# Weight difference in quarters, shared evacuations and a new order of all queues in a fused recurrence and maxout kernel

## The chip, the cores and the metric

The kernel runs on one core of a Trainium2 chip. The metric is device time in microseconds (us) of one execution; lower is better. A profiled execution also has a span (first to last instruction), some 1.7 us shorter than its time. A run more than 1.5% above the fastest of its kernel is called slow and is left out of all ratios; the medians quoted are of all runs, slow ones included.

## The reference

A gated recurrence over 768 time steps, for 4 batches and 8 heads of width 48, feeds a feed-forward layer with a maximum of two products:

```python
for t in range(S):                      # S = 768, per batch and head
    state = f[t][:, None] * state + outer(k[t], v[t])      # f = sigmoid(f_logit)
    y[t] = q[t] @ state
x = y as (3072, 384)
g = maximum(x @ w1, x @ w2)             # w1, w2: 384 x 1024
out = g @ w_out                         # 1024 x 384
```

The kernel uses max(a, b) = b + relu(a - b): out = relu(x @ (w1 - w2)) @ w_out + x @ (w2 @ w_out). So it needs the **difference** wd = w1 - w2 and the **product of the weights** m2 = w2 @ w_out, both computed on the chip.

## The kernel before

The time axis is cut into three windows for each of four batches: twelve "steps". All work is a list of words, issued to the five engines, each of which gets its own words in that order. The order is therefore in essence the schedule.

```python
# Lf, Lk, Lq, Lv: loads (SyncE queue)   W1, W2: row gathers of w1, w2 (GpSimd queue)   Wo: load of w_out
# E: two exponential passes (ScalarE)   e/g: pair sums es (GpSimd/VectorE)   C: cumulative sums (TensorE)
# X: five exponentials (ScalarE)        K/k, Q/q: kp, qp products (GpSimd/VectorE)   V/U: vb cast
# T: transposes (TensorE) + trs copies  A: at products (TensorE) + masking at_m (VectorE)
# S, Y: y products, xT copies           D, N: sadd products and new state
# wc, wT, wo, wm: cast w2, transpose it, cast w_out, product m2   ws: difference wd
# d g.fp: layer piece (h, relu into gT) o g.par: output piece   (a letter v, a, p after w.. names the engine)
ORDER = """
... V1 D0 S0 K1 W1:1 W2:1 W2:2 E2 Lf:3 N0 g2 W1:2 Lk:2 Lq:2 q1 D1 Z0 Y0 T1 N1 E3 e3 A1 wTa0 C2 S1 Lv:2
wcp1 C3 Wo:0 Z1 wcv2 Wo:1 Lf:4 X2 wsv0 wsv1 Y1 q2 X3 k2 Lk:3 wTa1 Lv:3 Lq:3 V2 wTv2 d0.0 d0.1 d0.2
d0.3 Lf:5 T2 wov0 d1.0 d1.1 wov2 Lk:4 d1.2 woa3 A2 Lv:4 D2 d1.3 Lq:4 Lf:6 wop1 E4 wma2 Lk:5 wma0 N2
g4 Q3 k3 wmv1 ...                                                               # (cut)
"""
def stage_T(s):                                   # (cut: 32 transposes into two PSUM banks)
    for h in range(2):
        nc.vector.tensor_copy(t[:, h], ps[h])
def stage_Y_act(s):                               # (cut)
    for h, ps in enumerate(ys.pop(s)):
        nc.scalar.copy(x[:, :, :, h, :], ps.rearrange("p j (a t) -> p j a t", a=2))
    for r in range(2):                            # fill the free rows of xT with the fourth head pair
        nc.scalar.dma_start(out=x[r * DP + D:(r + 1) * DP, 0:KT, :], in_=x[r * DP:r * DP + D, KT, :])
def piece_d(g, fp):                               # uses columns 256 fp .. 256 fp + 255 of wd
    for f in range(2):
        ff = 2 * fp + f
        for kt in range(KT):
            nc.tensor.matmul(out=ps[:, f, :], lhsT=wd[:, kt, ff * C:(ff + 1) * C], rhs=xT[g][:, kt, :], ...)
    nc.scalar.activation(gT[g][:, 2 * fp:2 * fp + 2, :], ps, AF.Relu)
def make_m2(kt, copy):
    for ff in range(FG):
        nc.tensor.matmul(out=ps, lhsT=w2T[:, ff, kt * C:(kt + 1) * C], rhs=wo[:, ff, :], ...)
    copy(m2[:, kt, :], ps)
def subtract(h, engine):
    cols = slice(h * d_ff // 2, (h + 1) * d_ff // 2)
    engine.tensor_sub(wd[:, :, cols], w1_f[:, :, cols], w2_f[:, :, cols])
```

## Time and profile before

| | before |
|---|---|
| time, median of 3 | 147.72 us (147.45 to 148.41) |
| span of the profiled run | 146.0 us |
| first layer piece (first h matmul) | 32.16 us |
| from there to the last matmul | 109.94 us, 0.56 us of it idle on TensorE |
| last eviction and store | 3.90 us |

The last three rows add up to the span. The views that give them are shown in the prediction. In a list of instructions, a line reads: start, length, engine, source line, operation, output<-inputs, shapes, count, and in brackets the idle time before it and what ended it.

### The profile page before, as it was taken

Reading aid. Unit: us, or ns where it says so; the run is one execution under the profiler, and the core shown is the slowest. Engines: PE = TensorE matmul, PEld = TensorE weight load, DVE = VectorE, ACT = ScalarE, POOL = GpSimd, SP = SyncE. Lnnn points to the kernel's source line nnn. Section 1 sums busy time; section 2 is a strip of 40 time slices with the busy share of each in tenths; the row PEclk is TensorE's granted clock in tenths of the full one; section 3 lists DMA queues with packets and bytes.
Section 4 is the critical chain, followed back from the end, with each engine's and each line's share of the span. In section 5 each row is a group of like instructions: output and inputs, shape, how many; then the busy total and the mean of one; then the engine's idle time right before and its main releaser. Section 6 shows DMA issues by size and latency. Waiting matters only on the chain.

```text
span 146.0 us, 5288 instructions
## 1 busy us (share of the span) xinstructions
PE 123.3 (84%) x2292; PEld 90.6 (62%) x2292; DVE 95.4 (65%) x179; ACT 89.9 (62%) x179; POOL 57.9 (40%) x68
## 2 busy tenths in 40 slices
PE   0017379649999999999999999999999999999990
PEld 0005267437866767876867676786857877866750
DVE  5157988479797697867893868957588751613030
ACT  3462947774797786969967886586526634650500
POOL 7376777220019475544206748286305610000000
PEclk9999999999999999999999999999999999999998
DMA  3999999999999004999999994993002301102022
GB/s 103 325 326 354 355 357 408 399 316 264 299 259 268 7 14 136 315 318 292 264 292 274 278 245 150 277 277 111 27 8 104 121 6 47 77 14 108 4 108 108
DMA packets 55128, 29.25 MB, mean 200 GB/s; under 512 B 50624, under 2 KB 52800, under 8 KB 55104
## 3 DMA queue, kind: packets, MB, share of 16 engines
q1 hardware_dynamic: 52704, 25.17, 59.7%
q0 software_dynamic: 864, 3.15, 5.3%
q10 hardware_dynamic: 1536, 0.59, 1.5%
q8 instruction: 18, 0.29, 0.8%
q14 instruction: 6, 0.05, 0.1%
HBM read 23.59 MB, written 4.72 MB: 194 GB/s over the span
## 4 chain that ended last, share of the span: by engine, by line
PE 63%; DMA 11%; POOL 7%; ACT 6%; DVE 6%; issue 4%; DVEq 0%
PE h L360 22%; PE o L373 18%; PE o L370 7%; DMA w_f<-in_moe_w_dram,row_of 6%; PE trp L236 4%; PE y L306 3%; DMA qt<-in_q_dram 3%; PE at L252 3%; PE y L286 3%; POOL kp L219 2%; DMA ft<-in_f_logit_dram 2%; POOL w_f L102 2%; ACT both L180 2%; PE sadd L320 1%; DVE wd L405 1%
## 5 line engine op out<-in xcount | busy, mean ns | idle before, releaser
L362 ACT ACTIVATE gT<-h 128x512 bf16<-128x512 f32 x48 | 28.0, 598 | 22.1 <-PE h L360 19.9
L360 PE MATMUL h<-xT,wd 128*128 128x256 bf16 x288 | 36.9, 281 | 2.3 <-DVE wd L405 1.9
L373 PE MATMUL o<-wo,gT 128*128 128x384 bf16 x192 | 35.1, 326 | 0.0
L264 DVE TENSOR_TENSOR at_m<-at,mask 128x512 bf16<-128x512 f32 x48 | 29.8, 683 | 5.3 <-PE at L252 5.3
L360 PEld LDWEIGHTS <-wd 128*128 128x128 bf16 x288 | 28.0, 101 | 8.4 <-DVE wd L405 2.2
L375 DVE COPY ob<-o 128x384 f32<-128x384 f32 x24 | 13.3, 556 | 21.8 <-PE o L373 21.8
L373 PEld LDWEIGHTS <-gT 128*128 128x128 bf16 x192 | 18.8, 98 | 12.4
L337 POOL TENSOR_TENSOR state<-tmp_s,f_last 128x256 bf16<-128x256 f32 x16 | 10.5, 657 | 37.2 <-DVE tmp_s L336 24.6
L219 POOL TENSOR_TENSOR kp<-kt,f_inv 128x768 bf16<-128x768 f32 x9 | 16.3, 1815 | 10.3 <-DMA kt<-in_k_dram 5.9
L239 DVE COPY trs<-trp 128x1024 bf16<-128x1024 bf16 x24 | 15.4, 685 | 3.4 <-PE trp L236 3.4
L370 PE MATMUL o<-m,xT 128*128 128x384 bf16 x72 | 15.7, 328 | 0.0
L344 ACT CAST xT<-y 128x512 bf16<-128x512 f32 x24 | 12.9, 591 | 3.9 <-PE y L306 3.9
L210 ACT ACTIVATE f_inv<-cum 128x384 f32<-128x384 f32 x12 | 5.9, 493 | 13.9 <-DVE even L201 9.8
L187 POOL TENSOR_TENSOR es<-both 128x384 bf16<-128x384 f32 x9 | 9.0, 999 | 8.7 <-issue 4.4
L180 ACT ACTIVATE both<-ft 128x768 f32<-128x768 f32 x12 | 10.2, 846 | 3.6 <-DMA ft<-in_f_logit_dram 2.2
L219 POOL TENSOR_TENSOR qp<-qt,f_dec 128x768 bf16<-128x768 f32 x6 | 11.6, 1939 | 0.0
L195 PE MATMUL cum<-es,u_inc 128*128 128x384 bf16 x12 | 4.6, 380 | 7.4 <-POOL es L187 7.4
L181 ACT ACTIVATE both<-both 128x768 f32<-128x768 f32 x12 | 10.1, 844 | 0.4
L201 DVE TENSOR_TENSOR even<-cum,both 128x384 f32<-128x384 f32 x12 | 6.6, 552 | 5.7 <-PE cum L197 5.1
L252 PE MATMUL at<-trs 48*64 48x128 bf16 x384 | 9.2, 234 | 1.3 <-DVE trs L239 1.3
L336 DVE TENSOR_TENSOR tmp_s<-sadd,state 128x256 f32<-128x256 f32 x16 | 6.8, 422 | 4.8 <-POOL state L337 3.0
L286 PE MATMUL y<-trs,state 48*64 48x128 bf16 x160 | 7.0, 226 | 2.6 <-DVE state L333 2.6
(64 smaller groups left out, 154.5 us busy)
## 6 DMA issues: line engine op xcount, KB each, us to landing
ft<-in_f_logit_dram SPq DMA_DIRECT2D x12, 384.0 KB, 5.6
vt<-in_v_dram SPq DMA_DIRECT2D x12, 384.0 KB, 5.6
kt<-in_k_dram SPq DMA_DIRECT2D x12, 384.0 KB, 5.5
qt<-in_q_dram SPq DMA_DIRECT2D x12, 384.0 KB, 5.1
out_dram<-ob SPq DMA_DIRECT2D x12, 384.0 KB, 2.5
wo_f<-in_moe_w_out_dram SPq DMA_DIRECT2D x2, 768.0 KB, 12.6
xT<-xT ACTq DMA_DIRECT2D x24, 24.0 KB, 3.2
w_f<-in_moe_w_dram,row_of POOLq DMA_INDIRECT x6, 6.4
```

Of the source, the lines that this page charges most:

```text
L180: nc.scalar.activation(flat(both), flat(loaded[s]["f"]), AF.Exp, bias=0.0, scale=-1.0)
L219: engine.tensor_mul(pad(nm + "p", s)[:, :, :, 0:D], by_parity(loaded[s][nm]), t.rearrange("p two (h d) -> p two h d", h=H))
L239: nc.vector.tensor_copy(t[:, h], ps[h])
L252: nc.tensor.matmul(out=ps[r][h * HC:(h + 1) * HC, j % 2, par, :], lhsT=t[rows, h, 0, j, par, :], rhs=t[rows, h, 1, j].rearrange("p a t -> ...
L264: nc.vector.tensor_mul(m[:, r, 2 * jj:2 * jj + 2], ps[r], mask.rearrange("p j a b t -> p j a (b t)"))
L286: nc.tensor.matmul(out=ys[s][h][r * DP:(r + 1) * DP, j, :], lhsT=st[rows, j, :], rhs=t[rows, h, 1, j].rearrange("p a t -> p (a t)"), start ...
L344: nc.scalar.copy(x[:, :, :, h, :], ps.rearrange("p j (a t) -> p j a t", a=2))
L360: nc.tensor.matmul(out=ps[:, f, :], lhsT=wd[:, kt, ff * C:(ff + 1) * C], rhs=xT[g][:, kt, :], start=(kt == 0), stop=(kt == KT - 1))
L362: nc.scalar.activation(gT[g][:, 2 * fp:2 * fp + 2, :], ps, AF.Relu)
L370: nc.tensor.matmul(out=ps, lhsT=xT[g][:, kt, cols], rhs=m2[:, kt, :], start=(kt == 0), stop=False)
L373: nc.tensor.matmul(out=ps, lhsT=gT[g][:, ff, cols], rhs=wo[:, ff, :], start=False, stop=(ff == FG - 1))
L375: nc.vector.tensor_copy(obs[g][:, par, :], ps)
```

## The change

The stated intent: cut the difference into quarters, so that a piece waits only for the 256 columns it uses; let ScalarE and VectorE share some evacuations; compute m2 before the first piece; and reorder every queue.

```diff
 ORDER = """
-Lf:0 E0 Lv:0 e0 C0 X0 Lk:0 V0 W2:0 Lf:1 K0 Lq:0 Lv:1 E1 q0 e1 T0 Lk:1 C1 Lf:2 W1:0 Lq:1 A0 X1 wca0
-V1 D0 S0 K1 W1:1 W2:1 W2:2 E2 Lf:3 N0 g2 W1:2 Lk:2 Lq:2 q1 D1 Z0 Y0 T1 N1 E3 e3 A1 wTa0 C2 S1 Lv:2
-wcp1 C3 Wo:0 Z1 wcv2 Wo:1 Lf:4 X2 wsv0 wsv1 Y1 q2 X3 k2 Lk:3 wTa1 Lv:3 Lq:3 V2 wTv2 d0.0 d0.1 d0.2
+Lf:0 E0 Lv:0 g0 Lk:0 Lf:1 W2:0 W2:1 E1 Lq:0 C0 X0 wca0 k0 U0 Lf:2 Lk:1 Lq:1 q0 Lv:1 e1 C1 X1 W2:2 K1
+Q1 W1:0 T0 Lf:3 D0 A0 Wo:1 Wo:0 N0 Lk:2 Lq:2 Lv:2 V1 E2 Lf:4 g2 W1:1 wca1 t1 Lk:3 E3 e3 D1 C2 N1 A1
+X2 Lf:5 wTv1 wTv0 wov3 wov0 S0 wov1 wca2 W1:2 C3 Z0 Lq:3 S1 Lv:3 Lk:4 woa2 Z1 Y0 Lq:4 K2 y1 wTv2 X3
+wmv0 wsv0 wma1 q2 wma2 wsp2 wsv1 T2 U2 d0.0 d0.1 Lv:4 Lk:5 E4 D2 Lq:5 N2 wsv3 A2 S2 Lv:5 d0.2 d0.3
+e4 K3 d1.0 Z2 o0.0 V3 E5 Y2 C4 Lf:6 Q3 e5 o0.1 X4 T3 D3 d1.1 K4 N3 d1.2 C5 V4 X5 d1.3 Q4 A3 d2.0 Q5
   (the rest of the list is reordered in the same way: cut)
-    def stage_T(s):
+    def stage_T(s, copy=nc.vector.tensor_copy):
-        for h in range(2):
-            nc.vector.tensor_copy(t[:, h], ps[h])
+        nc.vector.tensor_copy(t[:, 0], ps[0])
+        copy(t[:, 1], ps[1])
-    def stage_Y_act(s):
+    def stage_Y_act(s, copy=nc.scalar.copy):
-        for h, ps in enumerate(ys.pop(s)):
-            nc.scalar.copy(x[:, :, :, h, :], ps.rearrange("p j (a t) -> p j a t", a=2))
+        for h, (ps, fn) in enumerate(zip(ys.pop(s), (nc.scalar.copy, copy))):
+            fn(x[:, :, :, h, :], ps.rearrange("p j (a t) -> p j a t", a=2))
-    def subtract(h, engine):
-        cols = slice(h * d_ff // 2, (h + 1) * d_ff // 2)
+    def subtract(part, engine):
+        cols = slice(part * d_ff // 4, (part + 1) * d_ff // 4)
+        "t": lambda a: stage_T(int(a), nc.scalar.copy),                  # trs shared, 4 steps
+        "y": lambda a: (stage_Yv(int(a)), stage_Y_act(int(a), nc.vector.tensor_copy)),   # xT shared, 7 steps
```

More of the change, by code (lines that the diff above doesn't have):

```diff
@@ L17 @@
 ORDER = """
-Lf:0 E0 Lv:0 e0 C0 X0 Lk:0 V0 W2:0 Lf:1 K0 Lq:0 Lv:1 E1 q0 e1 T0 Lk:1 C1 Lf:2 W1:0 Lq:1 A0 X1 wca0
-V1 D0 S0 K1 W1:1 W2:1 W2:2 E2 Lf:3 N0 g2 W1:2 Lk:2 Lq:2 q1 D1 Z0 Y0 T1 N1 E3 e3 A1 wTa0 C2 S1 Lv:2
-wcp1 C3 Wo:0 Z1 wcv2 Wo:1 Lf:4 X2 wsv0 wsv1 Y1 q2 X3 k2 Lk:3 wTa1 Lv:3 Lq:3 V2 wTv2 d0.0 d0.1 d0.2
-d0.3 Lf:5 T2 wov0 d1.0 d1.1 wov2 Lk:4 d1.2 woa3 A2 Lv:4 D2 d1.3 Lq:4 Lf:6 wop1 E4 wma2 Lk:5 wma0 N2
-g4 Q3 k3 wmv1 C4 U3 S2 D3 Z2 N3 Lq:5 X4 o1.0 T3 E5 Y2 e5 o0.0 K4 C5 X5 A3 Lf:7 V4 S3 Q4 o0.1 T4 Z3
@@ L23 @@
-Lv:5 E6 Y3 Lf:8 D4 Lq:6 e6 Lk:6 N4 Lv:6 d2.0 o1.1 A4 K5 E7 S4 Z4 d2.1 Lq:7 d2.2 d2.3 Lf:9 Y4 V5 D5
-Lv:7 N5 d3.0 d3.1 g7 d3.2 C6 q5 Lf:10 o2.0 X6 K6 Lv:8 C7 X7 T5 o2.1 A5 S5 Lk:7 E8 Z5 e8 d3.3 U6 d4.0
-d4.1 C8 Y5 q6 q7 X8 Lk:8 K7 V7 o3.0 Lq:8 T6 d4.2 o3.1 d4.3 E9 E10 D6 e9 N6 A6 d5.0 o4.0 Lv:9 d5.1
-d5.2 d5.3 C9 e10 D7 N7 S6 Z6 Lf:11 X9 Lq:9 Lk:9 Lq:10 T7 Y6 Q8 o4.1 U9 Lk:10 A7 K8 V8 S7 o5.0 C10 Z7
-k9 E11 Lv:10 Y7 Lv:11 Lq:11 X10 D8 Q9 Lk:11 T8 o5.1 d6.0 d6.1 d6.2 A8 S8 Q10 D9 Z8 d6.3 d7.0 T9 Y8
@@ L28 @@
-o6.0 d7.1 K10 d7.2 A9 e11 T10 U10 d7.3 o6.1 C11 o7.0 X11 S9 Z9 D10 K11 A10 Y9 o7.1 d8.0 d8.1 d8.2
-V11 Q11 d8.3 S10 T11 Z10 D11 Y10 o8.0 d9.0 o8.1 d9.1 d9.2 d9.3 A11 S11 d10.0 Z11 d10.1 d10.2 Y11
-o9.0 d10.3 o9.1 o10.0 d11.0 d11.1 d11.2 d11.3 o10.1 o11.0 o11.1
+Lf:0 E0 Lv:0 g0 Lk:0 Lf:1 W2:0 W2:1 E1 Lq:0 C0 X0 wca0 k0 U0 Lf:2 Lk:1 Lq:1 q0 Lv:1 e1 C1 X1 W2:2 K1
+Q1 W1:0 T0 Lf:3 D0 A0 Wo:1 Wo:0 N0 Lk:2 Lq:2 Lv:2 V1 E2 Lf:4 g2 W1:1 wca1 t1 Lk:3 E3 e3 D1 C2 N1 A1
+X2 Lf:5 wTv1 wTv0 wov3 wov0 S0 wov1 wca2 W1:2 C3 Z0 Lq:3 S1 Lv:3 Lk:4 woa2 Z1 Y0 Lq:4 K2 y1 wTv2 X3
@@ new lines @@
+wmv0 wsv0 wma1 q2 wma2 wsp2 wsv1 T2 U2 d0.0 d0.1 Lv:4 Lk:5 E4 D2 Lq:5 N2 wsv3 A2 S2 Lv:5 d0.2 d0.3
+e4 K3 d1.0 Z2 o0.0 V3 E5 Y2 C4 Lf:6 Q3 e5 o0.1 X4 T3 D3 d1.1 K4 N3 d1.2 C5 V4 X5 d1.3 Q4 A3 d2.0 Q5
+Lf:7 d2.1 d2.2 D4 Lq:6 Lv:6 S3 Z3 V5 T4 Lq:7 N4 Lk:6 Lv:7 E6 d2.3 y3 o1.0 Lq:8 Lq:9 A4 K5 Lf:8 S4 Z4
+E7 e6 o1.1 C6 Y4 g7 D5 X6 T5 o2.0 Q6 Lk:7 C7 V6 N5 X7 o2.1 d3.0 Lf:9 d3.1 k6 d3.2 Lv:8 A5 D6 t6 d3.3
+N6 d4.0 d4.1 Q7 Lv:9 d4.2 d4.3 A6 S5 S6 Z5 E8 K7 Z6 y5 e8 V7 o3.0 o3.1 E9 Lf:10 D7 Lk:8 y6 Lk:9 C8
@@ L31 @@
+Lf:11 g9 o4.0 d5.0 N7 V9 Lv:10 X8 d5.1 C9 X9 V8 Lk:10 T7 o4.1 d5.2 Q8 d5.3 Lq:10 k8 K9 d6.0 t8 A7 D8
+o5.0 E10 Lv:11 S7 Z7 E11 A8 e10 q9 D9 Y7 o5.1 d6.1 d6.2 C10 d6.3 S8 e11 T9 Z8 X10 Lk:11 y8 o6.0 K10
+d7.0 d7.1 d7.2 Lq:11 q10 t10 A9 S9 U11 C11 d7.3 Z9 o6.1 o7.0 X11 y9 o7.1 Q11 U10 d8.0 K11 d8.1 d8.2
+d8.3 T11 D10 D11 A10 d9.0 d9.1 d9.2 o8.0 d9.3 A11 S10 Z10 S11 Z11 Y10 o8.1 y11 o9.0 o9.1 d10.0 d10.1
+d10.2 d10.3 d11.0 d11.1 d11.2 o10.0 d11.3 o10.1 o11.0 o11.1
 """
@@ L427 @@
         "V": lambda a: stage_V(int(a), nc.vector.tensor_copy), "U": lambda a: stage_V(int(a), nc.scalar.copy),
-        "T": attention(stage_T), "S": attention(stage_S), "Z": attention(stage_Z),
+        "T": attention(stage_T), "t": lambda a: stage_T(int(a), nc.scalar.copy),
+        "S": attention(stage_S), "Z": attention(stage_Z),
         "A": lambda a: (stage_A(int(a)), stage_A_dve(int(a))),
         "Y": lambda a: (stage_Yv(int(a)), stage_Y_act(int(a))),
+        "y": lambda a: (stage_Yv(int(a)), stage_Y_act(int(a), nc.vector.tensor_copy)),
         "D": lambda a: (stage_D(int(a)), stage_D_dve(int(a), 0)),
```

## The prediction

> **What bounds the kernel now.** I began with the page's busy row and its 40 slices, went on to the stretches (busy time by engine in chosen windows), then to the chain that ended last, and only then to the engines' timelines of the first 45 us.
>
> ```profile
> PE 123.3 (84%) x2292; PEld 90.6 (62%) x2292; DVE 95.4 (65%) x179; ACT 89.9 (62%) x179; POOL 57.9 (40%) x68
> ...
> PE   0017379649999999999999999999999999999990
> ...
> DMA  3999999999999004999999994993002301102022
> ```
>
> Busy shares are averages over two regimes. TensorE is filled in every slice from the tenth on and mostly empty before; the DMA is full from the second slice to the thirteenth. The cut by stretches, made at the start of the first layer piece (32.16 us) and at the end of the last matmul (142.10 us), says it exactly:
>
> ```profile
> 0.00:32.16 32.16, 13.93 (x316) 11.12 (x317) 20.60 (x52) 19.38 (x38) 18.95 (x35) 1.00 1.03 330
> 32.16:142.10 109.94, 109.38 (x1976) 79.51 (x1976) 74.29 (x127) 70.53 (x142) 38.92 (x33) 1.00 0.58 166
> 142.10:146.00 3.90, 0.00 (x0) 0.00 (x0) 0.56 (x1) 0.00 (x0) 0.00 (x0) 0.83 0.25 101
> ```
>
> The columns are the length, then busy us and count of PE, PEld, DVE, ACT and POOL, then clock, DMA share and GB/s. After 32.16 us TensorE idles 0.56 us in 110 us, so no engine there can be sped up to any effect. Before it TensorE has 18 us of idle time; after it stands a fixed end of 3.9 us (last eviction, last store). The chain shows what ends the empty stretch:
>
> ```profile
> 20.09 1.04 POOL w_f L102
> 21.14 0.63 POOL state L337
> 21.77 0.16 issue
> 21.93 8.14 DMA w_f<-in_moe_w_dram,row_of
> 30.07 0.03 issue
> 30.10 0.05 DVEq L405
> 30.15 0.04 issue
> 30.20 1.92 DVE wd L405
> 32.11 0.05 issue
> 32.16 4.37 PE h L360 x24
> ```
>
> The last gather of w1 is issued at 21.93 us, lands 8.14 us later, half of the weight difference is then subtracted in 1.92 us, and only then can the first piece (h) run. Everything TensorE does after that point, divided by its rate, is the rest of the kernel. One thing matters among it:
>
> ```profile
> 40.62 4.06 PE L399 MATMUL m2p<-wo,w2T 128*128 128x384 bf16 x24
> ```
>
> The product of the weights (w2 times w_out) is computed at 40.6 us, in the full stretch, although both its inputs were loaded by about 30 us.
>
> **What the skill says.** The Trainium skill, "TensorE: Matmul & The Clock Gate", Part 1, says that the array runs at half rate until it has been busy for some 3.4 us. The trace agrees: the first 24 h matmuls took 4.37 us, 182 ns each, while 18 later ones took 2.07 us in the chain, 115 ns each, and the page's clock row, which is the throttle's grant, shows nothing of it. "SBUF — State Buffer", Who interferes with whom, says VectorE with two SBUF inputs and GpSimd lock each other out for a whole instruction. The trace agrees: the qp product on VectorE takes 0.95 us as a rule, but 1.88 us at 10.10 us, where a kp product was running on GpSimd. "DMA: Bandwidth & Descriptors", Queues, rings and completion order, says engines take packets from the queues in turn, so a gather doesn't simply wait behind all queued loads. Here gathers landed in 5.3 to 8.4 us, the slow ones being those issued close together with the w_out load.
>
> **The change, part by part.** Nothing of the mathematics goes: 144 pairs of h matmuls, 24 o groups and all attention products stay.
>
> (1) **Product of the weights ahead of the pieces.** In the old order TensorE did, before the first piece, four cum products, two rounds each of transposes, at, sadd and both y products, and three w2 transposes. The new order has all of these too, and adds the three m2 products and the transposes of step 2. At the full rate these are 3 x 8 x 163 ns = 3.9 us (163 from 1.30 us per eight o matmuls in the chain; the trace shows about 4.06 us) and 0.57 us (the chain's transposes of one step). So at the first piece about 4.5 us less work remains.
>
> (2) **A warmer array.** The cold part of the first pieces costs 4.37 - 24 x 0.109 = 1.75 us (0.109 from 2.62 us per 24 late in the chain). In the new order the 24 products of 384 columns stand just before; they absorb the cold part, in time when the first piece waits for weights anyway. Gain about 1.75 us.
>
> (3) **When the first piece can start.** I followed the new queues by hand with durations of this trace. Two gathers of w2 go out at once at 4 us, since nothing is ahead of them on GpSimd. They take about 1.3 us each from the loads (524 KB at some 400 GB/s), so ft of step 1 lands near 8 us and qt of step 0 near 11. ScalarE: both1 8.2 to 9.9, the five exponentials of step 0 to 11.7, a cast and vb to 13.5, the exponentials of step 1 to 15.3. GpSimd: es1, the third w2 gather, kp1 14.5 to 16.3, qp1 to 18.1, the first w1 gather to 19.3, state, the second to 21. The transposes of step 1 then run at 18.1; ScalarE evicts one half by 20.2, does both3 by 21.9, GpSimd es3 by 22.9, a state product to 23.5, and the last w1 gather goes out at 23.7 us instead of 21.93. But the gathers are less bunched; with 5.5 to 8 us to landing it is there at 29.2 to 31.7, estimate 30.3. Then VectorE has a first quarter of the difference (1.83 / 2 = 0.92 us for half the width), qp2 (0.95) and the second quarter (0.92), while GpSimd takes the third in about 1.81 us (its time for a product of the same 768 elements), and the lock makes one wait for the other. In TensorE's order the transposes of step 2, which need qp2, stand ahead of the first piece. So transposes at about 33.6 and the first piece at 34.2 us, 2.0 later than now. The quarters alone save 1 us against waiting for halves; without them it would be worse.
>
> (4) **Shared evacuations.** Seven steps move one of two xT copies from ScalarE (0.54 us each) to VectorE (about 0.57), four move one trs copy (0.69) from VectorE to ScalarE (about 1.02, as its w2T copy of the same shape). Together with the moved casts and products this leaves VectorE at about 95.6 us, ScalarE at 90.3 and GpSimd at 60.5. No engine becomes the bound; it shortens latencies in a stretch where TensorE waits for nothing. I count 0.
>
> (5) **Full stretch.** The work is the same and its order is mixed anew. The old one had 0.56 us of idle; a new one can be as good, hardly better. I add 0.8 us, since fewer pieces are ready at once early on: two pieces, then step 2's attention, whose third and fourth pieces wait for quarters from GpSimd and VectorE.
>
> **Sum.** -4.5 (work done ahead) - 1.75 (cold rate) + 2.0 (later first piece) = -4.25; + 0.8 of new gaps = -3.45, which I widen to -3.45 to -4.5 as the late start may overlap with the last products. Span about 142.0, and 1.7 us on top, as now (147.7 for a span of 146.0): **143.6 us**, -2.8%.
>
> **Rivals.** (a) The gather lands later. Its queue place now depends on a chain of es3, step-1 products and states, each waiting for a load. A slip of 2 us in it goes one to one into the time: 145.6, called the same. For it: two gathers of w2 ahead of the loads push the first qt and the second ft back; against it: W1's last gather landed slowly before because three gathers and w_out were in flight together. (b) The full stretch gets holes: attention steps 2 to 5 bunch, at_m on VectorE (4 x 0.62 us) or GpSimd's kp and qp (1.8 us each) come late, and the loads behind stores in the one SyncE queue arrive late. Two or three us of holes: 145.5 to 146.5. For it: VectorE and ScalarE are 68 and 64% busy there; against: the old order shows the same mix with 0.56 us idle. (c) The gather lands as early as now and the start is at 32.2: full gain of 6, 141.5 us. For it: es0 and kp0 move to VectorE, so GpSimd is free earlier than I reckon if the loads land sooner; against it: GpSimd has two products more before its last gather.
>
> **Range and chances.** One us of doubt on the landing, one on the holes, some on the cold rate: 141.0 to 146.2 for 8 in 10. The limit for faster is 144.8 us. I give 0.72 to faster, 0.25 to the same, 0.03 to slower, as that would need over 7 us of new holes.
>
> **What would show it.** Right: the m2 products lie before the first h matmul and that first h group runs at about 115 ns a matmul, not 182; the last gather is issued at 23 to 25 us and lands at 29 to 32; the first h starts at 33 to 35; from there to the last matmul it is 104 to 106 us instead of 109.94, with at most 1.5 us idle; the end stays 3.9 us. Wrong: a last gather beyond 33 us, or TensorE waits of over 2 us after the first piece, by at_m, states, or loads stuck behind stores.

## The result and the profile after

The changed kernel took **144.34 us** (median of 4 runs, 143.71 to 146.32, the last one slow) against 148.06 us (4 runs, the three of the table above and one more) of the kernel before. The ratio of the fast runs is **0.9736**, 95% interval 0.9672 to 0.98: faster. Ratios here and below are the mean time of one kernel's fast runs over that of the other's in the same rounds, so they are not quite the ratio of the medians quoted.

The slices of the profile after, to be held against those of before:

```profile
PE   0107498994999999999999999999999999999980
...
PEclk9999999998699999999999999999999999999999
DMA  4999999999999499296990999938102200321022
```

TensorE is denser from the fifth slice on, then dips to 4 in the tenth; right behind the dip, the clock row falls to 8 and 6. The same three stretches as before, cut at the first h and at the last matmul (columns as in the prediction):

```profile
0.00:34.22 34.22, 18.79 (x373) 13.94 (x373) 24.53 (x59) 23.22 (x43) 21.16 (x34) 1.00 1.03 324
34.22:138.64 104.42, 103.95 (x1926) 76.29 (x1920) 72.94 (x126) 66.15 (x133) 42.79 (x34) 0.98 0.59 170
138.64:142.50 3.86, 0.00 (x0) 0.00 (x0) 0.55 (x1) 0.00 (x0) 0.00 (x0) 1.00 0.25 102
```

The first piece starts 2.06 us **later** than before, and 5.52 us less lies behind it; the end is unchanged. 2.06 - 5.52 = -3.46, the span's 146.0 to 142.5. The chain around the start (start, length, what):

```profile
23.80 6.45 DMA w_f<-in_moe_w_dram,row_of
...
30.37 0.96 DVE wd L405
31.33 2.50 DVE qp L219
33.83 0.05 issue
33.88 0.41 PE trp L236 x16
34.29 2.50 PE h L360 x12
```

The last gather goes out at 23.80 us and is there at 30.25. Then come one quarter of the difference (0.96 us), qp of step 2, and step 2's transposes, which stand ahead of the first piece in TensorE's order. Two things in it are wrong by their length. A qp product takes 0.95 us elsewhere on VectorE; here it took 2.50. And 12 h matmuls in 2.50 us are 208 ns each, where a run at full rate has about 110.

Where do the 5.52 us go? I took each matmul from its start to the next one's start, from the first h on, and summed by operation: m2 products 3.90 to 0; transposes 6.02 to 5.15; h 34.80 to 34.09; all others together within 0.1 us. That is -3.90, -0.87 and -0.71.

### The profile page after: what moved, and what is told of

It reads as the page before. It is cut to its first block, busy times and chain, and to the rows that moved or that the text cites. A ratio compares the mean times of both kernels' runs of the same rounds, so it can differ in the third digit from the quotient of the medians.

```text
span 142.5 us, 5301 instructions
## 1 busy us (share of the span) xinstructions
PE 122.7 (86%) x2292; PEld 90.2 (63%) x2292; DVE 98.0 (69%) x184; ACT 89.4 (63%) x176; POOL 63.9 (45%) x68
## 4 chain that ended last, share of the span: by engine, by line
PE 72%; DMA 13%; DVE 5%; ACT 3%; POOL 2%; SPq 1%; issue 1%; DVEq 0%
PE h L360 23%; PE o L373 22%; PE o L370 9%; DMA ft<-in_f_logit_dram 8%; DMA w_f<-in_moe_w_dram,row_of 5%; PE trp L236 4%; PE y L306 4%; PE at L252 3%; PE y L286 2%; PE sadd L320 2%; DVE qp L219 2%; SPq L93 1%; DVE wd L405 1%; PE cum L195 1%; DVE ob L375 1%
## 5 line engine op out<-in xcount | busy, mean ns | idle before, releaser
L360 PE MATMUL h<-xT,wd 128*128 128x256 bf16 x288 | 35.9, 278 | 0.2 <-DVE wd L405 0.2
L337 POOL TENSOR_TENSOR state<-tmp_s,f_last 128x256 bf16<-128x256 f32 x16 | 11.7, 732 | 25.4 <-DVE tmp_s L336 22.7
L219 POOL TENSOR_TENSOR qp<-qt,f_dec 128x768 bf16<-128x768 f32 x8 | 14.8, 1860 | 12.1 <-ACT f_last L213 12.1
L219 POOL TENSOR_TENSOR kp<-kt,f_inv 128x768 bf16<-128x768 f32 x9 | 17.0, 1888 | 7.1 <-DMA kt<-in_k_dram 4.9
L344 ACT CAST xT<-y 128x512 bf16<-128x512 f32 x17 | 9.5, 587 | 5.3 <-PE y L306 3.8
L238 DVE COPY trs<-trp 128x1024 bf16<-128x1024 bf16 x12 | 8.2, 686 | 6.1 <-PE trp L236 6.1
L197 PEld LDWEIGHTS <-es 128*128 128x128 bf16 x48 | 3.2, 103 | 9.5 <-issue 8.8
L306 PE MATMUL y<-at_m,vb 64*64 64x128 bf16 x384 | 8.4, 233 | 0.4 <-issue 0.4
L252 PEld LDWEIGHTS <-trs 48*64 48x64 bf16 x384 | 7.1, 121 | 2.1 <-issue 1.2
```

The lines of the kernel that those rows point to most:

```text
L219: engine.tensor_mul(pad(nm + "p", s)[:, :, :, 0:D], by_parity(loaded[s][nm]), t.rearrange("p two (h d) -> p two h d", h=H))
L252: nc.tensor.matmul(out=ps[r][h * HC:(h + 1) * HC, j % 2, par, :], lhsT=t[rows, h, 0, j, par, :], rhs=t[rows, h, 1, j].rearrange("p a t -> ...
L306: nc.tensor.matmul(out=ys[s][h][r * DP:(r + 1) * DP, j, :], lhsT=vb[rows, par, 2 * j + r, :], rhs=m[rows, r, j, par, :], start=first, stop ...
L337: nc.gpsimd.tensor_mul(new, tmp, f_last)
```

## The experiments

Twelve more runs were made, two of them repeats of a kernel, all with correct results. Those of one group ran on the same chip and share their runs of the kernel before.

### 1. What made qp slow: the third quarter moved to VectorE

GpSimd's third quarter ran beside qp. On GpSimd's and VectorE's timelines of the changed kernel:

```profile
30.41 2.60 POOL L405 TENSOR_TENSOR wd<-w_f 128x768 bf16<-128x768 f32 x1 [0.63 <-DMA w_f<-in_moe_w_dram,row_of]
```

```profile
31.25 2.57 DVE L219 TENSOR_TENSOR qp<-qt,f_dec 128x768 bf16<-128x768 f32 x1
```

Both have two inputs in SBUF, and both are slower than alone (GpSimd takes 1.81 us for the same 768 elements). GpSimd's started while VectorE's first quarter ran and ended at 33.01; the reading is that qp was held until then, for it ended 0.81 us later.

```diff
-... wma2 wsp2 wsv1 T2 U2 ... D2 Lq:5 N2 wsv3 A2 ...
+... wma2 wsv1 T2 U2 ... D2 Lq:5 N2 wsv2 wsv3 A2 ...
```

> The changed kernel with the third quarter of the weight difference moved from GpSimd to VectorE, just ahead of the fourth. Lock theory (the qp product of step 2 took 2.57 us instead of 0.95 because GpSimd's 2.60 us subtraction held the shared SBUF port): qp2 takes 0.95 us and ends near 32.3 us, TensorE's wait before the first piece shrinks from 2.0 to about 0.5 us, the first h starts near 32.7 us instead of 34.2, and as the gap is short the clock does not drop: another 1.5 us. Time about 141.5 us, minus whatever the third piece waits for its quarter (up to 0.9 us). Rival (qp2 is slow for another cause, such as late data): first h at 34.2 us still, time 144.3 us.

Measured: 142.91 us (6 runs, two of them slow), ratio 0.9627 (0.9581 to 0.9673). VectorE and TensorE of this run:

```profile
31.63 0.95 DVE L219 TENSOR_TENSOR qp<-qt,f_dec 128x768 bf16<-128x768 f32 x1
```

```profile
32.64 0.41 PE L236 MATMUL trp<-ident,qp 64*128 64x64 bf16 x16 [1.81 <-DVE qp L219]
32.98 1.48 PE L360 MATMUL h<-xT,wd 128*128 128x256 bf16 x12
```

qp is back at 0.95 us and the first piece starts 1.24 us earlier: the lock theory holds. The wait shrank only to 1.81 us, not to 0.5, because the m2 products ended earlier too (30.4 us). The 12 matmuls took 1.48 us, at full rate. The third and fourth pieces then waited 1.01 and 0.46 us for their quarters (the expectation had allowed up to 0.9), about what is missing to 141.5.

### 2. What halved the clock: filler in TensorE's wait

The changed kernel in 2 us stretches (columns as above; the seventh is the clock):

```profile
32.00:34.00 2.00, 0.12 (x8) 0.12 (x10) 2.00 (x2) 1.34 (x3) 1.01 (x1) 1.00 0.99 254
34.00:36.00 2.00, 2.00 (x26) 1.50 (x23) 1.89 (x3) 0.46 (x1) 0.00 (x0) 0.61 1.10 289
36.00:38.00 2.00, 2.00 (x72) 1.53 (x72) 0.46 (x2) 1.32 (x3) 0.00 (x0) 0.54 1.11 296
```

```diff
+    def junk(n):                       # result is never read
+        ps = bank("junk")[:, 0:HD]
+        for i in range(n):
+            nc.tensor.matmul(out=ps, lhsT=w2T[:, i % FG, 0:C], rhs=wo[:, i % FG, :], start=True, stop=True)
-... wsp2 wsv1 T2 ...
+... wsp2 wsv1 J12 T2 ...
```

> The changed kernel with 12 extra matmuls of 384 columns, whose result nobody reads, put into TensorE's 2 us wait before the second half of step 2's transposes. Idle-clock theory (the 2 us wait made the throttle halve the clock from 34.3 to 38 us): the granted clock stays 1.00 from 34 to 38 us, the first 12 h matmuls take 1.3 us instead of 2.5, and the time falls by about 1.5 us to 142.8 although work was added. Rival (the clock falls for another cause, such as load or a fixed phase): the clock row still shows 0.5 to 0.6 there and the time stays at 144.3 or rises by up to 0.3 us.

Measured: 142.98 us (6 runs, one of them slow), ratio 0.963 (0.9589 to 0.9671). TensorE, and two stretches:

```profile
32.01 2.11 PE L406 MATMUL junk<-wo,w2T 128*128 128x384 bf16 x12
...
34.63 1.48 PE L360 MATMUL h<-xT,wd 128*128 128x256 bf16 x12
```

```profile
24.00:30.00 6.00, 5.17 (x84) 3.55 (x84) 3.79 (x8) 3.38 (x8) 2.64 (x2) 0.72 1.10 361
...
34.00:36.00 2.00, 2.00 (x45) 1.61 (x44) 2.00 (x4) 0.51 (x1) 0.00 (x0) 1.00 1.01 259
```

The piece starts 0.41 us later than in the changed kernel, work was *added*, and by the ratios the kernel is 1.1% faster. With the wait filled, the clock stays at 1.00 behind it.

The other traces fit. Four fast ones have TensorE waits of 2.0 us or more once TensorE ran at full rate: the changed kernel (2.00 us), experiment 3 (3.29 and 3.60), experiment 4 (2.95) and the products alone in experiment 5 (2.88). In all four the clock falls to a half at the wait or at most 1.6 us after it. It does not fall behind a wait of 1.81 us (experiment 1) or of 1.42 (experiment 6). But the length of one wait is not the whole rule. In the filler run itself the clock was at a half from 25.60 to 29.01 us, over part of the products (4.94 us instead of 4.21), and in the 3.4 us at full rate before that no wait was over 0.8 us. And in one of the four fast runs of the control in experiment 4 the record lists a mean clock of 1.000 for the unaltered changed kernel (143.09 us, the others 144.12 to 145.20). So the filler shows that the half clock behind the wait could be avoided and what it cost; which idle time brings it on stays open.

### 3. The part said to gain: the m2 products put back behind four pieces

```diff
-wmv0 wsv0 wma1 q2 wma2 wsp2 wsv1 T2 ... d0.2 d0.3
+wsv0 q2 wsp2 wsv1 T2 ... d0.2 d0.3 wmv0 wma1 wma2
```

> The changed kernel with only the three products of the weights moved back behind the first four pieces. If doing them ahead is what gains (my step 1): the first h stays at 34 us, since the gather and qp2 set it, TensorE idles some 4 us more before it, and the time rises by 3.9 us or a little more (cold array) to 148 to 149 us, all of the gain lost. Rival (the new order of the full stretch or the shared evacuations make the gain): under 1 us of change, 144.3 to 145.3 us.

Measured: 148.37 us (4 runs, one of them slow), ratio 1.0005 (0.9946 to 1.0064): the whole gain is gone. TensorE:

```profile
33.99 0.61 PE L236 MATMUL trp<-ident,qp 64*128 64x64 bf16 x16 [3.60 <-DVE qp L219]
34.53 2.74 PE L360 MATMUL h<-xT,wd 128*128 128x256 bf16 x12
...
40.46 4.06 PE L399 MATMUL m2p<-wo,w2T 128*128 128x384 bf16 x24
```

The start did not move (34.5 against 34.2 us); the 3.9 us of products moved from a stretch in which TensorE otherwise waits into one in which it does not.

### 4. The sharing undone, on the changed kernel and on a steadier one

```diff
-... t1 ... y1 ... y3 ... t6 ... y5 ... y6 ... t8 ... y8 ... y9 ... t10 ... y11
+... T1 ... Y1 ... Y3 ... T6 ... Y5 ... Y6 ... T8 ... Y8 ... Y9 ... T10 ... Y11
```

> The changed kernel with all 11 shared evacuations undone (trs both on VectorE, xT both on ScalarE), order kept. My step 4 counts them as worth nothing: 144.0 to 144.8 us. Rival: they shorten the way to the first piece or fill holes later; then 1 to 3 us slower, 145.5 to 147.5 us, with TensorE waiting for trs or xT.

Measured: 145.91 us (6 runs, one of them slow), ratio 0.9804 (0.9747 to 0.986). To judge it I ran the changed kernel again in the next group:

> The changed kernel once more, unaltered, as the yardstick of this group: 144.3 us, ratio 0.974 to the kernel before, whichever theory holds. It also says whether the run without shared evacuations (145.9 us, ratio 0.980) was really slower: if this control comes out at 0.974 or less, the sharing is worth about 1 us and my zero for it was too low; if it comes out near 0.980, zero stands.

Measured: 144.78 us (6 runs, two of them slow; 144.24 without these), ratio 0.9738 (0.9666 to 0.9809). The intervals overlap, so this pair alone settles nothing. Sorted by the mean clock that the record lists for each fast run, it points to 1.5 us: at 0.998 or more 143.09 us with the sharing against 144.60 and 144.66 without, at 0.988 or less 143.71 to 145.20 against 145.71 to 146.56 (different chips, few runs). The pair was therefore repeated on the version of experiment 6, both on one chip:

> The pieces-first version once more, unaltered, as the yardstick for the next: 141.6 to 142.5 us. It is the better ground for judging the shared evacuations, since its runs lie closer together than those of the changed kernel, whose half-clock stretch varies from run to run.

> The pieces-first version with all 11 shared evacuations undone. My zero for the sharing: within 0.3 us of the yardstick beside it, some 142.0 us. Rival (sharing shortens chains that TensorE waits for, as the earlier run without it hinted with 1.0 to 1.5 us): 143.0 to 143.5 us, with added TensorE waits for trs, at_m or state after the first piece.

Measured: 142.0 us (141.67 to 142.99), ratio 0.9582 (0.9545 to 0.9619) with the sharing; 143.49 us (143.25 to 145.26), ratio 0.9709 (0.966 to 0.9757) without. **My zero was wrong**: the sharing is worth 1.5 us. In the profiles the first h starts almost together (32.32 and 32.46 us), and from there to the last matmul it is 104.1 against 105.4 us. Only 0.26 us of that shows as idle time (1.29 against 1.03 us); the rest is matmuls that follow each other more slowly. One wait that is listed is behind VectorE; TensorE at step 8, with the sharing and without:

```profile
87.49 0.58 PE L252 MATMUL at<-trs 48*64 48x128 bf16 x26
```

```profile
88.90 0.41 PE L252 MATMUL at<-trs 48*64 48x128 bf16 x15 [0.21 <-DVE at_m L264]
```

At that place the two versions differ by 0.7 us ahead of the transposes (84.49 against 83.83) and by 1.3 us after the y products (90.05 against 88.75). Summed by operation as above, at is 0.34, the state part of y 0.45 and h 0.35 us longer. That the evicting copies come later is the likely cause, but not shown: the single waits are mostly too short to be named in the trace.

### 5. Single parts of the change, put into the kernel before

The products alone, with their casts and copies:

```diff
-... Lf:4 X2 wsv0 wsv1 Y1 q2 X3 k2 Lk:3 wTa1 Lv:3 Lq:3 V2 wTv2 d0.0 ...   (wov0 wov2 woa3 wop1 wma2 wma0 wmv1 later)
+... Lf:4 X2 Y1 wTa1 wTv2 wov0 wov2 woa3 wop1 wsv0 wma2 wma0 wsv1 wmv1 q2 X3 k2 Lk:3 Lv:3 Lq:3 V2 d0.0 ...
```

> The kernel before with only the products of the weights, and the casts and copies that they need, moved ahead of the first piece; no other part of the change. Theory that the products gain only as far as they fill time that TensorE would wait anyway: the casts of w_out cannot start before it lands at 29.7 us and they hold up the weight difference on VectorE, so the first piece slips from 32.2 to 34 to 36 us while 3.9 us of work is gone behind it: 147.0 to 148.5 us, little or no gain. Rival (the products ahead gain their full 3.9 us by themselves): 144 us.

Measured: 154.28 us (153.56 to 155.18), ratio 1.0429 (1.0363 to 1.0494). I expected no gain; it is 6 us **slower**. TensorE:

```profile
33.48 5.71 PE L399 MATMUL m2p<-wo,w2T 128*128 128x384 bf16 x24 [1.25 <-DVE wo L394]
39.02 2.78 PE L360 MATMUL h<-xT,wd 128*128 128x256 bf16 x24
```

The w_out casts come late on VectorE (32.9 us), the products begin at 33.48 and run at a reduced rate (238 ns each; 4.06 us for 24 in the kernel before is 169), so the first piece starts at 39.02 us, 6.9 later than before. From there to the last matmul it is 109.3 us, hardly less than before, since the VectorE and ScalarE queues, shifted with it, leave TensorE 3.8 us of waits, 2.9 of them for one es. Behind that wait the clock is at a half from 50.49 to 53.91 us.

The quarters alone:

```diff
-... X2 wsv0 wsv1 Y1 ...
+... X2 wsv0 wsv1 wsv2 wsv3 Y1 ...
```

> The kernel before with only the weight difference cut into four quarters in the same place on VectorE. By my working the first piece starts 0.9 us earlier (31.2 instead of 32.2 us) and all else follows: time 0.9 us lower, 147.0 to 147.4 us where the kernel before shows 148. Rival (the first pieces run at half clock and wait for the next quarter each, so nothing comes of it): 0 to 0.3 us.

Measured: 147.62 us, ratio 0.9966 (0.9911 to 1.0022): no gain shown. The interval reaches down to a gain of 1.3 us, so my 0.9 us is neither shown nor excluded. In its trace the first h starts at 31.85 us and the first 24 h matmuls are done by 35.27, but then:

```profile
36.18 0.41 PE L236 MATMUL trp<-ident,kp 64*128 64x64 bf16 x16 [0.91 <-DVE kp L219]
```

VectorE has the whole difference, then qp, then kp of step 2, whatever the cut; the transposes start 0.28 us earlier than in the kernel before (36.46 us), and here no more came of it. But this trace is a disturbed one, and its run the slowest of the six (148.11 us, the others 147.43 to 147.79): in it, and in that of the products alone, TensorE stopped four times for 0.3 to 0.4 us between 19 and 24 us with nothing to wait for that the profile shows, which pushed at_m of step 1 from 23.0 to 25.7 us and the start of the difference from 30.20 to 30.84. I did not find out why. What the quarters gain in an undisturbed run stays open.

### 6. Towards a better version

Since experiments 1 and 2 say that the start is what is left, the first two pieces were put ahead of step 2's transposes, so that they do not wait for qp at all, and two more fill the waits of step 2 (all four quarters are on VectorE here):

```diff
-wmv0 wsv0 wma1 q2 wma2 wsp2 wsv1 T2 U2 d0.0 d0.1 Lv:4 Lk:5 E4 D2 Lq:5 N2 wsv3 A2 S2 ... d1.0 ... d1.1
+wmv0 wsv0 wma1 wsv1 wma2 U2 d0.0 d0.1 q2 wsv2 T2 d1.0 Lv:4 Lk:5 E4 D2 d1.1 Lq:5 wsv3 N2 A2 S2
```

> The changed kernel with all four quarters of the difference on VectorE and the first two pieces put ahead of step 2's transposes, so that the first h waits for one quarter only (ready at 31.3 us) and not for qp2; three more pieces fill the waits for step 2. If the start of the pieces and the clock govern: first h near 31.3 us instead of 32.7 to 34.2, no half clock, waits until 40 us under 1 us in all, time 140.5 to 141.5 us. Rival (holes come back later, as step 2's state and attention are later): TensorE waits of 1 us or more after 40 us, time 142.5 us or more.

Measured: 142.0 us (141.59 to 142.5), ratio **0.9588** (0.9532 to 0.9643). The first h started at 32.68 us, not at 31.3:

```profile
32.68 1.47 PE L360 MATMUL h<-xT,wd 128*128 128x256 bf16 x12 [1.42 <-ACT m L401]
```

To see whether that releaser is the true one, the exponentials ahead of it on ScalarE were moved:

```diff
-... y1 wTv2 X3 wmv0 ... U2 d0.0 d0.1 q2 ...
+... y1 wTv2 wmv0 ... U2 d0.0 d0.1 X3 q2 ...
```

> As the run with the pieces first, but with the five exponentials of step 3 moved on ScalarE from ahead of the evictions of the weights' product to behind the first two pieces. In that run the first h waited 1.4 us, to 32.7 us, put down to the eviction on ScalarE that ended at 32.6 us. ScalarE theory: the eviction now ends near 30.9 us, the first h starts at 31.4 us, where the first quarter and the last product are done, and the time falls by about 1.2 us to 140.8. Rival (the wait is really for the two small transfers that fill up xT, issued at 26.8 and 27.5 us and up to 5.0 us on the way): first h still near 32.6 us and 142.0 us.

Measured: 142.2 us, ratio 0.9601 (0.9556 to 0.9646). The first h starts at 32.27 us, while the last of the evictions on ScalarE only begins at 32.20 us and takes 0.48: it is not what h waits for. The wait is now put down to the small transfers that complete xT. But in this run the m2 products met the half clock (5.08 us instead of 4.06) and ended only at 32.16 us, so by itself it does not tell the transfers from the products. The repeat of the pieces-first version above, with the products done by 31.6 us, also names the transfers; its chain and TensorE:

```profile
27.40 4.79 DMA xT<-xT
```

```profile
32.32 1.47 PE L360 MATMUL h<-xT,wd 128*128 128x256 bf16 x12 [0.73 <-DMA xT<-xT]
```

The landings settle it. The second of the two transfers landed at 32.55 us in experiment 6's first run, at 32.19 in its repeat, at 32.14 in this run and at 32.33 in the run without sharing; in all four the first h started 0.13 us later.

Last, the gather of w1 issued 2.5 us earlier, on top of that:

```diff
-... W1:1 wca1 ... wca2 W1:2 C3 ...
+... W1:1 W1:2 wca1 ... wca2 C3 ...
```

> As the one before, with the last gather of w1 issued right behind the second, near 21.2 us instead of 23.8. If the landing of the weights still bounds the start: quarters ready 1.5 to 2.5 us earlier, yet the three products keep TensorE until about 31.3 us, so the first h starts there with no wait, 140.5 us or a little less. If the gather only swaps places with loads in the full DMA: kt and qt of step 2 land later, the start of the pieces does not move by more than 0.3 us, and the time is that of the run before, or 0.5 us more.

Measured: 142.2 us, ratio 0.9598 (0.9553 to 0.9643), the first h at 32.00 us. It is the second case expected: kp of step 2 waited for its load until 29.3 us instead of 28.1, and the start gained 0.27 us, nothing in time. The gather landed at 28.89 us, but its gain seems to have gone into the lock of experiment 1 again: with kp on GpSimd from 29.30 to 31.11 us, the first quarter on VectorE took 2.06 us (29.87 to 31.93) instead of 0.96. The quarter, the transfers (31.86 us) and the products (31.95 us) were ready within 0.1 us of each other, so this run does not say which of them bounds the start. The last two versions are not shown to differ from the pieces-first version, which stays the fastest by its median (142.0 us).

## Why the prediction was right

The time (143.6 predicted, 144.34 measured) and the direction were right. By its steps:

- **Products ahead** (-3.9 and -0.57): right. -3.90 and -0.87 in the sum by operation, and experiment 3 loses the whole gain by moving the products alone. Experiment 5 adds what the prediction had not said: the same move without the reordered queues costs 6 us, because the products then stand on the path to the first piece instead of beside it.
- **Warmer array** (-1.75): the step that failed. The prediction listed "that first h group runs at about 115 ns a matmul, not 182" as a mark of being right; it ran at 208. The products did reach full rate (4.21 us for 24), but behind them came the 2.0 us wait for qp, and from 34.44 us the clock was at a half again. h gained 0.71 us in all, 1.04 us less than forecast. Experiment 2, where the clock holds behind the wait, is 1.4 us faster by the medians, enough for the missing part.
- **Start of the first piece** (34.2 us): right to 0.02 us, with the gather out at 23.80 (23.7 predicted) and landed at 30.25 (30.3). The lock between GpSimd and VectorE was named there and is confirmed by experiment 1. What was missed is that the products would be done by 31.5 us, so that the delay left TensorE idle, and the clock fell behind that. The side remark that quarters alone save 1 us is neither shown nor excluded by experiment 5, for the old order.
- **Shared evacuations** (0): wrong; 1.5 us in experiment 4.
- **New gaps in the full stretch** (+0.8): they did not come, 0.47 us of idle against 0.56. Without sharing the idle is 1.11 us in experiment 4, so this error and the one before may be one: the new order does bring gaps, and the sharing closes them. This is argued, not shown; in the repeated pair the idle differs by 0.26 us only.

The warm array was counted about 1 us too favourably and the gaps about 1 us too harshly; the two cancelled by luck, so the total is better than its parts. The bare sum (-3.45) is nearer to the span's -3.5 than the widened one from which the 143.6 us came. Rivals (a) and (b), a late gather and holes in the full stretch, did not occur; (c), a start at 32.2 us with the full gain, is nearly what the pieces-first version reaches (32.3 to 32.7 us, 142.0 us).

## What to carry to other kernels

Work moved ahead of a start gains only what it fills of an otherwise idle stretch, and the same move loses when the queues have not made its inputs ready: replay each engine's queue by hand to the first moment at which the bounding engine runs without pause, then count what is left behind that moment. Look at who else runs when a freshly split operation is spread over two engines: a GpSimd subtraction beside a VectorE product, both with two inputs in SBUF, cost more here (1.6 us on VectorE) than it took over (0.95). And a wait of TensorE can cost more than its length: behind the 2 us wait the 12 h matmuls took 2.57 us instead of 1.48, so that even useless matmuls in it paid.

## What the Trainium skill lacked or had wrong

- "TensorE: Matmul & The Clock Gate", Part 1, gives about 3.4 us of idle as what drops the clock. Here a wait of 2.00 us was followed by a granted clock of 0.61 and 0.54 over the next 4 us, and with the wait filled it stayed at 1.00. Waits of 1.81 us (experiment 1) and 1.42 us (experiment 6) did not drop it, yet in two traces it fell at 25.60 us (filler) and 25.72 us (exponentials later) though no wait in the 3.4 us at full rate before was over 0.8 us. The page does say that its window runs freely, which may explain a drop after less. One thing fits it: in five fast traces each stretch at half clock lasted 3.41 or 3.42 us, and in a sixth (experiment 3) 6.83, twice that. How much idle time in such a window drops the clock stays open.
- No page says what the profile's clock row shows before its first recorded change. In the kernel before it reads 1.00 while 24 h matmuls take 182 ns each, against 115 a little later; the durations show the slow start, the clock does not.
- "SBUF — State Buffer", Who interferes with whom, was right on the lock; the cost here was 1.6 us on VectorE (0.95 to 2.57) and 0.8 us on GpSimd (1.81 to 2.60), and 1.1 us on VectorE in the last run of experiment 6 (0.96 to 2.06).
- No page that I read treats the stops of 0.3 to 0.4 us in TensorE's issue, four of them between 19 and 24 us in the two traces of experiment 5; their cause stays open.
